# Third query tile, batch 2's scaling and the next queries' loads moved to other places in a linear attention + GEGLU kernel

## The chip, the cores and the metric

The kernel runs on one core of one Trainium2 chip. The metric is the device time of one execution in microseconds (us). Before the change the first three runs had a median of 329.17 us (328.63 to 329.31). The granted TensorE clock was between 0.997 and 1.000.

## The reference

For each of 8 batches and 8 heads (576 tokens of 64 features) a linear attention is computed; its output, laid out as 4,608 tokens of 512 features, goes through a gated feed-forward block.

```python
pos = np.arange(S); theta = np.pi / 2.0 * pos / S          # S = 576
def phi(x): r = np.maximum(x, 0.0); return concat([r * cos(theta), r * sin(theta)], axis=-1)
q_p, k_p = phi(q), phi(k)
kv  = einsum('bhsf,bhsd->bhfd', k_p, v);  z = k_p.sum(axis=2)
x   = einsum('bhsf,bhfd->bhsd', q_p, kv) / (einsum('bhsf,bhf->bhs', q_p, z)[..., None] + 1e-06)
x   = x.transpose(0, 2, 1, 3).reshape(B * S, H * D)        # 4608 x 512
out = (gelu(x @ w_gate) * (x @ w_val)) @ w_out             # 512 -> 1536 -> 512
```

## The kernel before

The feed-forward work is cut into nine blocks of tokens (block 0 has 576, the others 512 or fewer). While block n runs its gate and value matmuls, the attention of batch n + 1 is slipped in between, so that its rows of x are ready for block n + 1. Every engine executes its own instructions in program order, so the place of a call in the program is its place in the engine's queue. These are the pieces that the change moves:

```python
def scale(f, j, which, eng, ...):         # sq(j, which, eng) for queries, sk for keys
    if eng == "v": nc.vector.tensor_scalar(d, s, col, 0.0, op0=ALU.mult, op1=ALU.max)
    else:          nc.scalar.activation(d, s, AF.Relu, scale=col)

def q_by_pe(b, j, bank, eng):             # turn one query tile on TensorE, 8 heads
    ...nc.tensor.transpose(out=qb[:, h, :], in_=qp[:, j, h, :], identity=ident)...
    if eng is not None: q_evac(b, j, bank, eng)     # PSUM -> SBUF on VectorE ("v") or ScalarE ("s")

def norm(xb, bank, g0, g1):               # VectorE: den + eps, reciprocal, numerator * reciprocal
def x_by_pe(b, t, xb, bank, eng):         # turn one tile of x on TensorE, evict it to xT
def turn_x(b, t, xb):                     # the same by a DMA transpose (later batches)

def gate(n, jt, c0, w, gb):               # 4 matmuls into bank gb, then ScalarE: gel = Gelu(bank)
def value(n, jt, c0, w, vb):              # 4 matmuls into bank vb, then VectorE:
    nc.vector.tensor_mul(hT[n % 2][...], gel[:, 0:w], ps[:, vb, 0:w])    # "the product"
```

A value matmul writes bank 6 or 7, and the product on VectorE reads it. The next value matmul into the same bank must wait until that product is done. The start of block 0 before the change:

```python
    x_by_pe(0, 0, x0, 4, "s", 0, 2)
    dummies(2, 5)                         # matmuls that only keep TensorE busy
    x_by_pe(0, 0, x0, 4, "s", 2, 4)
    # [cut]  X(t, ...) is x_by_pe of batch 0; Y(t, ...) is its numerator and norm
    sq(2, 0, "v"), sq(2, 1, "s")
    gate(0, 0, 0, 128, 5)
    gate(0, 1, 0, 128, 4)
    X(1, 2, "s")()
    sq(3, 0, "v"), sq(3, 1, "v")
    dummies(1, 7)
    q_by_pe(0, 2, 3, "v")
    value(0, 0, 0, 128, 6)
    value(0, 1, 0, 128, 7)
    gate(0, 0, 128, 128, 5)
    gate(0, 1, 128, 128, 4)
    sq(4, 1, "s"), sq(4, 0, "v")
    q_by_pe(0, 3, 0, "s")                 # 8 transposes between the gates and the values
    value(0, 0, 128, 128, 6)              # needs the product of value(0, 0, 0, 128, 6)
```

In blocks 1 to 6 small pieces are hung behind the twelve gate-and-value units of a block. In block 1 (n = 1) the attention of batch 2 has its steps after units 5 to 10; step i + 1 ends with the DMA transpose of x tile i. Block 2's first gate reads 448 rows of batch 2, so it needs tile 3, the transpose behind unit 9.

Of the kernel before, what the change touches and what calls it, by code (L numbers as in the profile page):

```python
# [16 lines left out]
def kernel(  # L17
# [12 lines left out]
    B, H, S, D = q.shape  # L30
# [6 lines left out]
    NJ = 4  # L37
# [86 lines left out]
    def dummies(n, bank=7):  # L124
        for _ in range(n):
            nc.tensor.matmul(ps[:, bank, :], lhsT=junk[:, 0:128], rhs=junk, start=True, stop=True)  # L126


    def scale(f, j, which, eng, h0=0, h1=H):
        dst, src = f  # L130
        col = (cos_c if which == 0 else sin_c)[:, j:j + 1]
        s, d = src[:, h0:h1, j, :], dst[:, j, h0:h1, which * D:(which + 1) * D]
        if eng == "v":
            nc.vector.tensor_scalar(d, s, col, 0.0, op0=ALU.mult, op1=ALU.max)  # L134
        else:
            nc.scalar.activation(d, s, AF.Relu, scale=col)  # L136
# [30 lines left out]
    def numer_mm(b, t, bank, g, rows=128):  # L167
        for h in range(4 * g, 4 * g + 4):
            nc.tensor.matmul(  # L169
                ps[0:rows, bank + g, (h % 4) * (D + 1):(h % 4 + 1) * (D + 1)],  # L170
                lhsT=qT[b % 2][:, t, h, 0:rows],
                rhs=kv[b % 2][:, h, 0:D + 1],
                start=True, stop=True,
            )

    def norm(xb, bank, g0, g1, rows=128):

        n = g1 - g0
        nd = ps[0:rows, bank + g0:bank + g1, 0:4 * (D + 1)].rearrange("p g (h e) -> p g h e", e=D + 1)
        den = rot.tile([128, 2, 4], FP32, name="den")  # L180
        nc.vector.tensor_scalar(den[0:rows, 0:n], nd[:, :, :, D], EPS, None, op0=ALU.add)
        rec = rot.tile([128, 2, 4], FP32, name="rec")
        nc.vector.reciprocal(rec[0:rows, 0:n], den[0:rows, 0:n])  # L183
        nc.vector.tensor_tensor(  # L184
            xb[0:rows, g0:g1], nd[:, :, :, 0:D],
            rec[0:rows, 0:n, :, None].to_broadcast([rows, n, 4, D]), op=ALU.mult,
        )
# [4 lines left out]
    def numer(b, t, bank, rows=128):  # L192

        numer_mm(b, t, bank, 0, rows)
        numer_mm(b, t, bank, 1, rows)
        xb = new_xb()
        norm(xb, bank, 0, 2, rows)
        return xb
# [14 lines left out]
    def gate(n, jt, c0, w, gb):  # L213

        p0 = starts[n] + c0
        for ct in range(CT):
            nc.tensor.matmul(  # L217
                ps[:, gb, 0:w], lhsT=wg_sb[:, ct, jt * 128:(jt + 1) * 128],
                rhs=xT[:, ct, p0:p0 + w], start=(ct == 0), stop=(ct == CT - 1),
            )  # L220
        gels[n, jt, c0] = gel = rot.tile([128, 512], FP32, name="gel", bufs=3)
        nc.scalar.activation(gel[:, 0:w], ps[:, gb, 0:w], AF.Gelu)  # L222

    def value(n, jt, c0, w, vb):

        p0 = starts[n] + c0
        for ct in range(CT):
            nc.tensor.matmul(  # L228
                ps[:, vb, 0:w], lhsT=wv_sb[:, ct, jt * 128:(jt + 1) * 128],
                rhs=xT[:, ct, p0:p0 + w], start=(ct == 0), stop=(ct == CT - 1),  # L230
            )
        gel = gels.pop((n, jt, c0))
        nc.vector.tensor_mul(hT[n % 2][:, jt, 64 + c0:64 + c0 + w], gel[:, 0:w], ps[:, vb, 0:w])  # L233

    def gv_unit(n, jt, c0, w, gb, vb, mid=()):
        gate(n, jt, c0, w, gb)
        for f in mid:
            f()
        value(n, jt, c0, w, vb)
# [15 lines left out]
    def o_part(n, m, bank, j0, j1):  # L255
        c0 = 128 * m - starts[n] + 64
        for jt in range(j0, j1):
            nc.tensor.matmul(  # L258
                ps[:, bank, :], lhsT=hT[n % 2][:, jt, c0:c0 + 128], rhs=wo_sb[:, jt, :],
                start=(jt == 0), stop=(jt == JT - 1),  # L260
            )
        if j1 == JT:
            o_store(m, bank)
# [21 lines left out]
    def o_store(m, bank):  # L285
        o_sb = rot.tile([128, C], FP32, name="o_sb", bufs=4)
        nc.scalar.copy(o_sb, ps[:, bank, :])  # L287
        if (128 * m) % S % 128 == 0 and (128 * m) % S < 512:
            nc.sync.dma_start(out=rows_ap(128 * m, 128), in_=o_sb)
        else:  # L290
            nc.sync.dma_start(out=rows_ap(128 * m, 64), in_=o_sb[0:64])
            nc.sync.dma_start(out=rows_ap(128 * m + 64, 64), in_=o_sb[64:128])
# [26 lines left out]
    def q_by_pe(b, j, bank, eng, h0=0, h1=H):  # L319

        qb = ps[:, bank, :].bitcast(BF16).rearrange("p (h t) -> p h t", h=H)
        for h in range(h0, h1):
            nc.tensor.transpose(out=qb[:, h, :], in_=qp[:, j, h, :], identity=ident)  # L323
        if eng is not None:
            q_evac(b, j, bank, eng, h0, h1)

    def q_evac(b, j, bank, eng, h0=0, h1=H):
        qb = ps[:, bank, :].bitcast(BF16).rearrange("p (h t) -> p h t", h=H)
        cp = nc.vector.tensor_copy if eng == "v" else nc.scalar.copy
        if j < NJ:  # L330
            cp(qT[b % 2][:, j, h0:h1], qb[:, h0:h1])  # L331
        else:
            cp(qT[b % 2][:, j, h0:h1, 0:64], qb[:, h0:h1, 0:128:2])

    def x_by_pe(b, t, xb, bank, eng, c0=0, c1=CT, every=1):
        p0 = b * S + t * 128
        cp = nc.vector.tensor_copy if eng == "v" else nc.scalar.copy
        xb2 = xb.rearrange("p g h d -> p (g h d)")
        rows = 128 if t < NJ or every == 2 else 64
        view = ps[:, bank, 0:256].bitcast(BF16).rearrange("p (c t) -> p c t", c=CT)  # L340
        for ct in range(c0, c1):
            nc.tensor.transpose(  # L342
                out=view[:, ct, 0:rows], in_=xb2[0:rows, ct * 128:(ct + 1) * 128], identity=ident[0:rows, 0:rows],
            )
        cp(xT[:, c0:c1, p0:p0 + rows // every], view[:, c0:c1, 0:rows:every])

    def sq(j, which, eng, *h):
        scale(Q, j, which, eng, *h)
# [30 lines left out]
    norm(x0, 6, 0, 1)  # L379
    dummies(1, 4)  # L380
    numer_mm(0, 0, 6, 1)
    norm(x0, 6, 1, 2)
    numer_mm(0, 1, 0, 0)
    numer_mm(0, 1, 0, 1)
    norm(x1, 0, 0, 2)
    x_by_pe(0, 0, x0, 4, "s", 0, 2)
    dummies(2, 5)
    x_by_pe(0, 0, x0, 4, "s", 2, 4)

    nc.gpsimd.tensor_copy(tiny[0:1, 1:2], x0[0:1, 1, 3, D - 1:D])  # L390
    load_w(8, 12)
# [2 lines left out]
    A, Bw = (0, 256), (256, 320)  # L394
    xs = {1: x1}

    def X(t, bank, eng):
        return lambda: x_by_pe(0, t, xs[t], bank, eng)

    def Y(t, bank):  # L400
        def f():
            xs[t] = numer(0, t, bank, 128 if t < NJ else 64)
        return f

    sq(2, 0, "v"), sq(2, 1, "s")
    gate(0, 0, 0, 128, 5)
    gate(0, 1, 0, 128, 4)
    X(1, 2, "s")()
    sq(3, 0, "v"), sq(3, 1, "v")
    dummies(1, 7)  # L410
    q_by_pe(0, 2, 3, "v")
    value(0, 0, 0, 128, 6)
    value(0, 1, 0, 128, 7)
    gate(0, 0, 128, 128, 5)
    gate(0, 1, 128, 128, 4)
    sq(4, 1, "s"), sq(4, 0, "v")
    q_by_pe(0, 3, 0, "s")
    value(0, 0, 128, 128, 6)
    value(0, 1, 128, 128, 7)
    Y(2, 2)()  # L420
    q_by_pe(0, 4, 1, "s")
    gv_unit(0, 2, *A, 4, 6)
    X(2, 0, "s")()
    Y(3, 2)()
# [5 lines left out]
    gv_unit(0, 0, 384, 128, 4, 6)  # L430
    gv_unit(0, 1, 384, 128, 5, 7)
    X(4, 0, "v")()
    gv_unit(0, 4, *A, 3, 1)
    gv_unit(0, 2, *Bw, 4, 6)
    gv_unit(0, 3, *Bw, 5, 7)
    gv_unit(0, 0, 512, 64, 0, 3)
    gv_unit(0, 1, 512, 64, 1, 2)


    load_q(1, nc.gpsimd)  # L440
# [7 lines left out]
    def L(f, *a):  # L448
        return lambda: f(*a)
# [54 lines left out]
    y4 = numer(1, 4, 0)  # L504
    o_part(0, 3, 5, 5, 10)
    x_by_pe(1, 3, y[3], 7, "s")
    o_part(0, 3, 5, 10, 12)
    x_by_pe(1, 4, y4, 6, "v", every=2)

    def attn_step(b, i):  # L510

# [8 lines left out]
    for n in range(1, 7):  # L520
        b = n + 1
        a = after[n]

        def put(u, *fs):
            a[u].extend(fs)

        put(0, L(sq, 0, 0, "v"), L(sq, 1, 0, "v"), L(sq, 1, 1, "v"), L(sq, 0, 1, "s"))
        put(1, L(sq, 2, 0, "v"), L(sq, 2, 1, "s"), L(turn_q, b, 0, 3))
        put(1, L(sq, 3, 0, "v"), L(sq, 4, 0, "v"), L(sq, 4, 1, "v"), L(sq, 3, 1, "s"), L(turn_q, b, 3, 5))
        put(2, L(sk, 0, 0, "v"), L(sk, 1, 0, "v"), L(sk, 0, 1, "s"), L(sk, 1, 1, "s"))  # L530
        put(3, L(sk, 2, 0, "v"), L(sk, 3, 0, "v"), L(sk, 4, 0, "v"))
        put(3, L(sk, 2, 1, "s"), L(sk, 3, 1, "s"), L(sk, 4, 1, "s"), L(cast_v, b, 0, 4))
        put(4, L(cast_v, b, 4, 8, "s"))
        put(5, L(attn_step, b, 0))
        if b + 1 < B:

            for f, u in zip((load_q, load_k, load_v), (3, 4, 5) if n > 1 else (6, 11, 11)):
                put(u, L(f, b + 1))
        for i in range(5):
            put(6 + i, L(attn_step, b, i + 1))  # L540

    for n in range(2, NB):
        for i, m in enumerate(o_tiles_of(n - 1)):
# [47 lines left out]
```

## Time and profile before

| | before |
|---|---|
| median of the first 3 runs | 329.17 us |
| profiled span | 326.8 us |
| PE busy | 97% |
| PE's listed waits after the start-up (0.85 + 0.35 + 0.24 + 0.20) | about 1.6 us |
| the same with the dummy matmul that the change drops (0.22 us) | about 1.9 us |

The part of the page with busy time, share of the span and instruction count of each engine (PE is TensorE's matmuls, PEld its weight loads, DVE VectorE, ACT ScalarE):

```profile
PE 317.6 (97%) x2223; PEld 167.0 (51%) x2223; DVE 171.8 (53%) x382; ACT 150.6 (46%) x270; POOL 21.2 (6%) x41
```

The Trainium skill ("Perfetto Trace Analysis", Identifying the Most-Contended Engine) warns that matmul busy share alone does not tell how close TensorE is to its limit. So the pace is checked as well, in the chain of work that ended last (start in us, us, what, number of instructions):

```profile
60.66 0.86 PE ps L228 x4
61.52 0.86 PE ps L217 x4
```

Four matmuls of 512 columns take 0.86 us, 216 ns each. The Trainium skill ("TensorE: Matmul & The Clock Gate", Back-to-back issue gap) has a formula that for 512 columns comes to 512 / 2.4 + 2.5 = 215.8 ns; it calls this the gap of an isolated matmul, and says that in a stream of weight loads and matmuls the formula counts too much (131 ns measured there). This trace is such a stream, and it runs at 216 ns: the measurement agrees with the formula and not with the 131 ns. The groups shown follow one another without a hole at this pace; here the busy share does mean what it seems to mean. Busy time by stretch (stretch, length, then busy us and instructions of each engine) shows how little is idle once the first blocks are over:

```profile
16.40:25.80 9.40, 9.16 (x144) 8.13 (x144) 8.33 (x26) 6.29 (x16) 3.97 (x6) 1.00 1.30 207
84.00:312.00 228.00, 227.90 (x1409) 110.96 (x1410) 111.04 (x223) 99.31 (x167) 8.63 (x13) 1.00 0.62 149
```

From 84 to 312 us PE is idle 0.1 us of 228. In the first stretch VectorE (third pair of numbers) is busy 8.33 of 9.40 us: in this one place it is nearly as full as PE. What is left to win stands in PE's list of waits (engine, line, what it waited for, us in total, times, longest):

```profile
PE ps L126 <- DVE par_i L103: 1.7, 1, 1.7
PE ps L323 <- ACT qp L136: 1.0, 1, 1.0
PE ps L217 <- DMA xT<-xb: 0.8, 1, 0.8
PE ps L217 <- ACT xT L345: 0.3, 1, 0.3
PE ps L228 <- DVE hT L233: 0.2, 1, 0.2
PE ps L217 <- ACT gel L222: 0.2, 1, 0.2
```

The first two belong to the start-up and the change doesn't touch them. The third is the wait at block 2's first gate, seen in the timeline (start, us, engine, line, operation, tiles, and in brackets the idle time before it and its releaser). SPq is the queue that issues DMAs; the transpose of x tile 3 is issued at 80.96 us, and PE resumes at 83.97 us:

```profile
80.96 1.60 SPq L204 DMA_TRANSPOSE xT<-xb  x1
...
83.97 1.02 PE L217 MATMUL ps<-xT,wg_sb 128*128 128x512 bf16 x4 [0.85 <-DMA xT<-xb]
```

And this is the start of block 0, where the change moves most. (In the timelines of this document only the lines that matter are shown; others between them are left out, also where no dots stand.) DVE L233 is the product, L134 a scaling, L331 the eviction of turned queries; ACT L345 evicts turned x; PE L126 is a dummy, L323 a query turn:

```profile
16.38 0.49 PE L217 MATMUL ps<-xT,wg_sb 128*128 128x128 bf16 x6 [0.35 <-ACT xT L345]
16.94 0.38 PE L126 MATMUL ps<-junk 128*128 128x512 bf16 x1
17.17 0.60 ACT L345 COPY xT<-ps 128x512 bf16<-128x512 bf16 x1
...
18.45 0.47 DVE L233 TENSOR_TENSOR hT<-gel,ps 128x128 bf16<-128x128 f32 x2
18.50 0.61 PE L323 MATMUL ps<-ident,qp 128*128 128x128 bf16 x8
18.94 0.61 PE L228 MATMUL ps<-xT,wv_sb 128*128 128x128 bf16 x8
```

The two first products (x2) run at 18.45 to 18.92 us. PE passes that time with the turn of query tile 3, and its second pair of value matmuls starts at 18.94 us without a wait.

### The profile page before, as it was taken

Reading aid. Unit: us, or ns where it says so; the run is one execution under the profiler, and the core shown is the slowest. Engines: PE = TensorE matmul, PEld = TensorE weight load, DVE = VectorE, ACT = ScalarE, POOL = GpSimd, SP = SyncE. Lnnn points to the kernel's source line nnn. Section 1 sums busy time; section 2 is a strip of 40 time slices with the busy share of each in tenths; the row PEclk is TensorE's granted clock in tenths of the full one; section 3 lists DMA queues with packets and bytes.
Section 4 is the critical chain, followed back from the end, with each engine's and each line's share of the span. In section 5 each row is a group of like instructions: output and inputs, shape, how many; then the busy total and the mean of one; then the engine's idle time right before and its main releaser. Section 6 shows DMA issues by size and latency. Waiting matters only on the chain.

```text
span 326.8 us, 5867 instructions
## 1 busy us (share of the span) xinstructions
PE 317.6 (97%) x2223; PEld 167.0 (51%) x2223; DVE 171.8 (53%) x382; ACT 150.6 (46%) x270; POOL 21.2 (6%) x41
## 2 busy tenths in 40 slices
PE   7799999999899999999999999999999999999994
PEld 3497866555345544544454445444544444444443
DVE  5894776678753667365835484548455222322210
ACT  6574664772474256424652375237622332223321
POOL 2640010000100010001000010001000100100000
PEclk9999999999999999999999999999999999999999
DMA  7999999997699948993699359994523211000024
GB/s 226 284 205 275 205 298 306 316 182 173 189 270 270 299 103 158 301 267 81 129 305 290 81 101 216 357 135 84 144 51 79 44 37 34 32 32 32 35 64 96
DMA packets 87739, 55.42 MB, mean 170 GB/s; under 512 B 52512, under 2 KB 82976, under 8 KB 87712
## 3 DMA queue, kind: packets, MB, share of 16 engines
q1 hardware_dynamic: 81200, 48.71, 60.2%
q0 software_dynamic: 6080, 5.90, 10.1%
q10 hardware_dynamic: 432, 0.46, 0.4%
q8 instruction: 17, 0.28, 0.4%
q14 instruction: 10, 0.08, 0.1%
HBM read 37.75 MB, written 9.44 MB: 144 GB/s over the span
## 4 chain that ended last, share of the span: by engine, by line
PE 93%; DMA 3%; DVE 1%; ACT 1%; issue 1%; POOL 0%; SPq 0%; DVEq 0%; POOLq 0%; ACTq 0%
PE ps L217 28%; PE ps L228 28%; PE ps L258 28%; PE ps L169 3%; PE ps L153 3%; DMA qf<-in_q_dram 2%; PE ps L323 1%; DMA xT<-xb 1%; PE ps L342 1%; PE ps L276 1%; DVE vx L140 0%; SPq L79 0%; DVE hT L233 0%; DVE qT L331 0%; DVE xb L184 0%
## 5 line engine op out<-in xcount | busy, mean ns | idle before, releaser
L233 DVE TENSOR_TENSOR hT<-gel,ps 128x512 bf16<-128x512 f32 (+5 forms) x126 | 76.4, 610 | 129.4 <-PE ps L228 127.8
L217 PE MATMUL ps<-xT,wg_sb 128*128 128x512 bf16 (+5 forms) x504 | 113.7, 348 | 1.4 <-DMA xT<-xb 0.8
L228 PE MATMUL ps<-xT,wv_sb 128*128 128x512 bf16 (+5 forms) x504 | 113.6, 349 | 0.2 <-DVE hT L233 0.2
L222 ACT ACTIVATE gel<-ps 128x512 f32<-128x512 f32 (+5 forms) x126 | 67.5, 536 | 77.6 <-PE ps L217 75.7
L258 PE MATMUL ps<-wo_sb,hT 128*128 128x512 bf16 x420 | 96.5, 379 | 0.0
L228 PEld LDWEIGHTS <-wv_sb 128*128 128x128 bf16 x504 | 47.8, 98 | 46.4 <-issue 0.4
L217 PEld LDWEIGHTS <-wg_sb 128*128 128x128 bf16 x504 | 45.8, 98 | 41.8 <-issue 2.1
L258 PEld LDWEIGHTS <-hT 128*128 128x128 bf16 x420 | 40.0, 98 | 45.4
L287 ACT COPY o_sb<-ps 128x512 f32<-128x512 f32 x35 | 20.5, 586 | 75.2 <-PE ps L258 75.2
L184 DVE TENSOR_TENSOR xb<-ps,rec 128x512 bf16<-128x512 f32 (+2 forms) x41 | 27.8, 678 | 1.7 <-DVE rec L183 0.2
L136 ACT ACTIVATE kp<-kf,sin_c 128x512 bf16<-128x512 f32 (+1 forms) x41 | 25.4, 679 | 0.4 <-DMA kf<-in_k_dram 0.4
L134 DVE TENSOR_SCALAR qp<-qf,cos_c 128x512 bf16<-128x512 f32 x40 | 20.5, 553 | 0.0
L169 PEld LDWEIGHTS <-qT 128*128 128x128 bf16 (+1 forms) x320 | 15.0, 98 | 8.7 <-issue 1.9
L134 DVE TENSOR_SCALAR kp<-kf,cos_c 128x512 bf16<-128x512 f32 (+1 forms) x45 | 18.7, 463 | 1.0 <-DMA kf<-in_k_dram 1.0
L136 ACT ACTIVATE qp<-qf,sin_c 128x512 bf16<-128x512 f32 x27 | 18.5, 712 | 0.0
L169 PE MATMUL ps<-kv,qT 128*128 128x65 bf16 (+1 forms) x320 | 16.5, 193 | 0.2
L208 POOL COPY xT<-xr 128x256 bf16<-128x256 bf16 x6 | 2.4, 403 | 201.0 <-DMA xr<-xb 201.0
L153 PEld LDWEIGHTS <-kp 128*128 128x128 bf16 x320 | 10.9, 97 | 2.6 <-issue 0.7
L126 PE MATMUL ps<-junk 128*128 128x512 bf16 x35 | 9.9, 424 | 1.7 <-DVE par_i L103 1.7
L153 PE MATMUL ps<-vx,kp 128*128 128x65 bf16 x320 | 11.1, 193 | 0.1
L140 ACT CAST vx<-vf 128x1280 bf16<-128x1280 f32 (+1 forms) x9 | 9.7, 1074 | 1.2 <-DMA vf<-in_v_dram 1.2
L244 POOL COPY hT<-hT 128x768 bf16<-128x768 bf16 x8 | 7.6, 948 | 36.8 <-DVE hT L233 36.8
(55 smaller groups left out, 88.9 us busy)
## 6 DMA issues: line engine op xcount, KB each, us to landing
out_dram<-o_sb SPq DMA_DIRECT2D x38, 128.0 KB, 2.4
kf<-in_k_dram SPq DMA_DIRECT2D x7, 640.0 KB, 7.5
out_dram<-o_sb SPq DMA_DIRECT2D x16, 256.0 KB, 3.4
qf<-in_q_dram SPq DMA_DIRECT2D x6, 640.0 KB, 6.2
vf<-in_v_dram SPq DMA_DIRECT2D x6, 640.0 KB, 9.1
kf<-in_k_dram SPq DMA_DIRECT2D x7, 512.0 KB, 6.4
qf<-in_q_dram SPq DMA_DIRECT2D x6, 512.0 KB, 5.4
vf<-in_v_dram SPq DMA_DIRECT2D x6, 512.0 KB, 8.0
```

Source lines behind the costliest of these rows:

```text
L126: nc.tensor.matmul(ps[:, bank, :], lhsT=junk[:, 0:128], rhs=junk, start=True, stop=True)
L134: nc.vector.tensor_scalar(d, s, col, 0.0, op0=ALU.mult, op1=ALU.max)
L136: nc.scalar.activation(d, s, AF.Relu, scale=col)
L153: nc.tensor.matmul(ps[:, bank, (h % 4) * (D + 1):(h % 4 + 1) * (D + 1)], lhsT=kp[:, j, h, :], rhs=vx[b % 2][:, j, h, 0:D + 1], start=(j == ...
L169: nc.tensor.matmul(ps[0:rows, bank + g, (h % 4) * (D + 1):(h % 4 + 1) * (D + 1)], lhsT=qT[b % 2][:, t, h, 0:rows], rhs=kv[b % 2][:, h, 0:D ...
L184: nc.vector.tensor_tensor(xb[0:rows, g0:g1], nd[:, :, :, 0:D], rec[0:rows, 0:n, :, None].to_broadcast([rows, n, 4, D]), op=ALU.mult,)
L217: nc.tensor.matmul(ps[:, gb, 0:w], lhsT=wg_sb[:, ct, jt * 128:(jt + 1) * 128], rhs=xT[:, ct, p0:p0 + w], start=(ct == 0), stop=(ct == CT - 1),
L222: nc.scalar.activation(gel[:, 0:w], ps[:, gb, 0:w], AF.Gelu)
L228: nc.tensor.matmul(ps[:, vb, 0:w], lhsT=wv_sb[:, ct, jt * 128:(jt + 1) * 128], rhs=xT[:, ct, p0:p0 + w], start=(ct == 0), stop=(ct == CT - 1),
L233: nc.vector.tensor_mul(hT[n % 2][:, jt, 64 + c0:64 + c0 + w], gel[:, 0:w], ps[:, vb, 0:w])
L258: nc.tensor.matmul(ps[:, bank, :], lhsT=hT[n % 2][:, jt, c0:c0 + 128], rhs=wo_sb[:, jt, :], start=(jt == 0), stop=(jt == JT - 1),)
L287: nc.scalar.copy(o_sb, ps[:, bank, :])
```

## The change

It has three parts. In block 0's start the third query tile is scaled and turned earlier, in the hole of 0.35 us; the dummy goes; x tile 1 and the turned query tile 4 are evicted by VectorE instead of ScalarE, one scaling goes the other way, the turn of query tile 3 moves behind the value matmuls, and tile 4's gate and value are split. In block 1 a part of batch 2's query scaling is done before the block, and every attention step comes one unit earlier (as do two of the next loads). In blocks 2 to 5 the loads of the next queries go between the two turns of q (block 6 has no next queries to load: `b + 1 < B`).

```diff
--- before.py
+++ after.py
@@ -379,13 +379,16 @@
     norm(x0, 6, 0, 1)
     dummies(1, 4)
     numer_mm(0, 0, 6, 1)
+    sq(2, 1, "s")
     norm(x0, 6, 1, 2)
+    sq(2, 0, "v")
     numer_mm(0, 1, 0, 0)
     numer_mm(0, 1, 0, 1)
     norm(x1, 0, 0, 2)
     x_by_pe(0, 0, x0, 4, "s", 0, 2)
     dummies(2, 5)
     x_by_pe(0, 0, x0, 4, "s", 2, 4)
+    q_by_pe(0, 2, 3, None)
 
     nc.gpsimd.tensor_copy(tiny[0:1, 1:2], x0[0:1, 1, 3, D - 1:D])
     load_w(8, 12)
@@ -402,23 +405,21 @@
             xs[t] = numer(0, t, bank, 128 if t < NJ else 64)
         return f
 
-    sq(2, 0, "v"), sq(2, 1, "s")
     gate(0, 0, 0, 128, 5)
     gate(0, 1, 0, 128, 4)
-    X(1, 2, "s")()
-    sq(3, 0, "v"), sq(3, 1, "v")
-    dummies(1, 7)
-    q_by_pe(0, 2, 3, "v")
+    X(1, 2, "v")()
+    q_evac(0, 2, 3, "v")
+    sq(3, 0, "v"), sq(3, 1, "s")
     value(0, 0, 0, 128, 6)
     value(0, 1, 0, 128, 7)
     gate(0, 0, 128, 128, 5)
     gate(0, 1, 128, 128, 4)
     sq(4, 1, "s"), sq(4, 0, "v")
-    q_by_pe(0, 3, 0, "s")
     value(0, 0, 128, 128, 6)
     value(0, 1, 128, 128, 7)
     Y(2, 2)()
-    q_by_pe(0, 4, 1, "s")
+    q_by_pe(0, 3, 0, "s")
+    q_by_pe(0, 4, 1, "v")
     gv_unit(0, 2, *A, 4, 6)
     X(2, 0, "s")()
     Y(3, 2)()
@@ -430,11 +431,12 @@
     gv_unit(0, 0, 384, 128, 4, 6)
     gv_unit(0, 1, 384, 128, 5, 7)
     X(4, 0, "v")()
-    gv_unit(0, 4, *A, 3, 1)
+    gate(0, 4, *A, 3)
     gv_unit(0, 2, *Bw, 4, 6)
     gv_unit(0, 3, *Bw, 5, 7)
-    gv_unit(0, 0, 512, 64, 0, 3)
-    gv_unit(0, 1, 512, 64, 1, 2)
+    value(0, 4, *A, 1)
+    gv_unit(0, 0, 512, 64, 0, 2)
+    gv_unit(0, 1, 512, 64, 4, 6)
 
 
     load_q(1, nc.gpsimd)
@@ -504,8 +506,11 @@
     y4 = numer(1, 4, 0)
     o_part(0, 3, 5, 5, 10)
     x_by_pe(1, 3, y[3], 7, "s")
+    x_by_pe(1, 4, y4, 6, "v", every=2)
+    for j in range(NJ + 1):
+        sq(j, 0, "v")
     o_part(0, 3, 5, 10, 12)
-    x_by_pe(1, 4, y4, 6, "v", every=2)
+    sq(0, 1, "s")
 
     def attn_step(b, i):
 
@@ -524,20 +529,28 @@
         def put(u, *fs):
             a[u].extend(fs)
 
-        put(0, L(sq, 0, 0, "v"), L(sq, 1, 0, "v"), L(sq, 1, 1, "v"), L(sq, 0, 1, "s"))
-        put(1, L(sq, 2, 0, "v"), L(sq, 2, 1, "s"), L(turn_q, b, 0, 3))
-        put(1, L(sq, 3, 0, "v"), L(sq, 4, 0, "v"), L(sq, 4, 1, "v"), L(sq, 3, 1, "s"), L(turn_q, b, 3, 5))
-        put(2, L(sk, 0, 0, "v"), L(sk, 1, 0, "v"), L(sk, 0, 1, "s"), L(sk, 1, 1, "s"))
-        put(3, L(sk, 2, 0, "v"), L(sk, 3, 0, "v"), L(sk, 4, 0, "v"))
-        put(3, L(sk, 2, 1, "s"), L(sk, 3, 1, "s"), L(sk, 4, 1, "s"), L(cast_v, b, 0, 4))
-        put(4, L(cast_v, b, 4, 8, "s"))
-        put(5, L(attn_step, b, 0))
+        s = 0 if n > 1 else -1
+        if n > 1:
+            put(0, L(sq, 0, 0, "v"), L(sq, 1, 0, "v"), L(sq, 1, 1, "v"), L(sq, 0, 1, "s"))
+            put(1, L(sq, 2, 0, "v"), L(sq, 2, 1, "s"), L(turn_q, b, 0, 3))
+            put(1, L(sq, 3, 0, "v"), L(sq, 4, 0, "v"), L(sq, 4, 1, "v"), L(sq, 3, 1, "s"))
+            if b + 1 < B:
+                put(1, L(load_q, b + 1))
+            put(1, L(turn_q, b, 3, 5))
+        else:
+            put(0, L(sq, 1, 1, "s"), L(sq, 2, 1, "v"), L(turn_q, b, 0, 3))
+            put(0, L(sq, 3, 1, "v"), L(sq, 4, 1, "s"), L(turn_q, b, 3, 5))
+        put(2 + s, L(sk, 0, 0, "v"), L(sk, 1, 0, "v"), L(sk, 0, 1, "s"), L(sk, 1, 1, "s"))
+        put(3 + s, L(sk, 2, 0, "v"), L(sk, 3, 0, "v"), L(sk, 4, 0, "v"))
+        put(3 + s, L(sk, 2, 1, "s"), L(sk, 3, 1, "s"), L(sk, 4, 1, "s"), L(cast_v, b, 0, 4))
+        put(4 + s, L(cast_v, b, 4, 8, "s"))
+        put(5 + s, L(attn_step, b, 0))
         if b + 1 < B:
 
-            for f, u in zip((load_q, load_k, load_v), (3, 4, 5) if n > 1 else (6, 11, 11)):
+            for f, u in ((load_k, 3), (load_v, 5)) if n > 1 else ((load_q, 5), (load_k, 10), (load_v, 11)):
                 put(u, L(f, b + 1))
         for i in range(5):
-            put(6 + i, L(attn_step, b, i + 1))
+            put(6 + s + i, L(attn_step, b, i + 1))
 
     for n in range(2, NB):
         for i, m in enumerate(o_tiles_of(n - 1)):
```

## The prediction

> **What bounds the kernel now.** TensorE. The table of engines shows PE busy 317.6 of 326.8 us (97%), VectorE 53%, ScalarE 46%. In the chain of waits four matmuls of 512 columns take 0.864 us, 216 ns each. The Trainium skill ("TensorE: Matmul & The Clock Gate", Back-to-back issue gap) gives columns / 2.4 GHz + 2.5 ns, 215.8 ns; the trace agrees. From 84 to 312 us (busy time by stretch) PE is idle 0.1 us of 228. Only idle PE time elsewhere can be won.
>
> PE's list of waits: 1.7 us at the start and 1.0 us for the first scaled queries (untouched), 0.35 us at 16.4 us for ScalarE's eviction of turned x, 0.24 us at 25.2 and 0.20 us at 29.6 us for PSUM banks, and 0.85 us at 84.0 us, where block 2's first gate matmul waits for a DMA transpose of batch 2 (2.88 us, landing 83.8). With the removed dummy matmul (0.22 us) the change can reach about 1.9 us, 0.6%.
>
> **What the change does.**
> 1. Block 1 (batch 2). Query scaling partly goes before the block: five VectorE scalings of 0.48 us and one on ScalarE (0.71 us), where VectorE has idle time. The attention steps move one unit earlier, 1.7 us (gate and value) to 2.0 us (with a numerator). The transpose that landed too late should land over 1 us early. Gain 0.85 us, on the path. VectorE's first product is delayed about 0.5 us, inside the double-buffered banks' slack. The last x transpose, moved before two output matmuls, may wait 0.1 us for its input.
>
> 2. Block 0 start. The third query tile is turned earlier, filling the 0.35 us hole and removing a dummy. But VectorE is nearly full from 16.5 to 25 us, and its queue is in order. It gets x tile 1's eviction (0.42 us) and tile 4's query eviction (about 0.4 us), gives up one scaling (0.47 us), and does one scaling before tile 1's normalization, which ends near 17.1 instead of 16.6 us. My hand estimate from these durations: the first two products come at 19.0-19.5 instead of 18.45-18.9 us. The next value matmuls need their banks, and without the query turn that stood there, PE waits up to 0.8 us at about 18.5 us. Net, PE is about 0.3 us later at 21 to 26 us (range 0.3 earlier to 0.7 later). Tile 4's split gate and value trades the 0.20 us wait at 29.6 us for a similar one behind a product: nothing.
>
> 3. Later blocks: the next queries' loads (issue 1.3 us) go between the two turns of q. The second turn is delayed a few us, but is first used at unit 9, over 10 us later; PE waited for no load there. Value: zero.
>
> **Prediction.** -0.85 + 0.1 + 0.3 = -0.45 us: 328.7 us, 8 in 10 between 327.6 and 329.7. Faster by over 2%: 0.5%; within 2%: 98.5%; slower: 1%.
>
> **What would show it.** PE's wait for the x transpose at 84 us is gone. Between 17 and 26 us PE shows new waits of 0.3 to 1 us on VectorE's products, and block 0's output matmuls (now at 45.3 us) begin 0 to 0.6 us later. Batch 2's transposes issue 1.5 to 2 us earlier. Afterwards PE is as gapless as before, 216 ns a matmul, clock near 1.00.
>
> **What would make it wrong.** If VectorE keeps up at 17 to 20 us, hole and dummy are both won and the time falls by up to 1.9 us. If the loads beside the second query turn delay the transposes of x past a block's start, waits on DMA of 1 us or more appear in blocks 2 to 6. If batch 2's queries land after about 60 us, VectorE stalls at the start of block 1.

## The result, and the profile after

In the first four runs the changed kernel had a median of 328.95 us (328.66 to 329.21) against 328.90 us before (4 runs), ratio 1.0001, 95% interval 0.9984 to 1.0019. A ratio is the mean time of one kernel's fast runs over the mean of the other's in the same rounds, so it isn't quite the ratio of the medians that are quoted. Five more runs (the eighth experiment) gave 328.87 against 328.82 us, ratio 1.0000, interval 0.9986 to 1.0013. The kernel is as fast as before. The predicted 328.7 us lies 0.2 us away, inside the runs' spread. Part of this closeness is luck: the forecast was a drop of 0.45 us from 329.17 us, the kernel before came out at 328.90 us in the result's rounds, and the measured difference is +0.05 us.

The busy line of the page after:

```profile
PE 316.1 (97%) x2188; PEld 167.1 (51%) x2222; DVE 172.2 (53%) x383; ACT 150.5 (46%) x269; POOL 21.6 (7%) x41
```

A trap lies here. PE seems to have 35 matmuls and 1.5 us less. The program dropped only one matmul, the dummy, as the count of weight loads shows (2,222 for 2,223). The other 34 records are missing from this trace; a second trace of the same program had all 2,222, and 318.3 us busy. So I compare where instructions start, not busy sums. PE's list of waits after:

```profile
PE ps L126 <- DVE par_i L103: 1.7, 1, 1.7
PE ps L323 <- ACT qp L136: 1.3, 1, 1.3
PE ps L228 <- DVE hT L233: 0.8, 2, 0.6
PE ps L169 <- DVE xb L184: 0.3, 1, 0.3
```

The wait for the transpose of x and those for ScalarE (the eviction of x, a Gelu) are gone. In their place stand 0.8 us behind VectorE's products (0.56 of it new) and 0.3 us of a numerator matmul behind VectorE's normalization, which nobody had forecast. The timeline of block 0's start:

```profile
16.52 0.45 PEld L323 LDWEIGHTS <-qp 128*128 128x128 bf16 x8 [0.28 <-DVE qp L134]
16.52 0.62 PE L323 MATMUL ps<-ident,qp 128*128 128x128 bf16 x8
16.81 0.69 DVE L184 TENSOR_TENSOR xb<-ps,rec 128x512 bf16<-128x512 f32 x1
17.56 0.40 PE L342 MATMUL ps<-ident,xb 128*128 128x128 bf16 x4
17.99 0.42 DVE L345 COPY xT<-ps 128x512 bf16<-128x512 bf16 x1 [0.49 <-PE ps L342]
18.33 0.68 DVE L331 COPY qT<-ps 128x1024 bf16<-128x1024 bf16 x1
...
18.93 0.48 DVE L134 TENSOR_SCALAR qp<-qf,cos_c 128x512 bf16<-128x512 f32 x1
19.32 0.48 DVE L233 TENSOR_TENSOR hT<-gel,ps 128x128 bf16<-128x128 f32 x2
19.65 0.61 PE L228 MATMUL ps<-xT,wv_sb 128*128 128x128 bf16 x8 [0.56 <-DVE hT L233]
```

VectorE now has eviction, eviction, scaling and only then the products, back to back from 17.99 us. Just before, it is not busy but blocked: the normalization of x tile 1 (L184) ends at 17.50 us, and VectorE stands idle for 0.49 us, because next in its order is the eviction of x tile 1, which PE (L342) turns only at 17.56 us. The query eviction behind it could have run, since its turn on PE was over. The value matmuls at 19.65 us then wait 0.56 us. Nor is the old hole really filled: the query turn's weight loads waited 0.28 us for its scaling on VectorE, and start at 16.52 us. Now block 2's first gate; nothing stands in brackets:

```profile
80.53 1.38 SPq L204 DMA_TRANSPOSE xT<-xb  x1
...
84.26 1.03 PE L217 MATMUL ps<-xT,wg_sb 128*128 128x512 bf16 x4
```

And the place of the new numerator wait, in block 1:

```profile
71.26 1.03 PE L228 MATMUL ps<-xT,wv_sb 128*128 128x512 bf16 x4
71.46 0.60 ACT L222 ACTIVATE gel<-ps 128x512 f32<-128x512 f32 x1 [0.49 <-PE ps L217]
72.76 0.69 DVE L233 TENSOR_TENSOR hT<-gel,ps 128x512 bf16<-128x512 f32 x1 [2.23 <-PE ps L169]
...
74.54 0.42 PE L169 MATMUL ps<-kv,qT 128*128 128x65 bf16 x8 [0.27 <-DVE xb L184]
```

The value matmuls end at 71.26 + 1.03 = 72.29 us and the Gelu at 72.06 us, so the product could start at about 72.35 us. It starts at 72.76 us, with VectorE idle. The bracket names a matmul that the product does not need, which is how this view looks when no recorded event explains a start. In the trace, the product's wait for PE is passed at 72.33 us, and then nothing happens for 0.43 us.

To see where time comes and goes without the scatter of the first loads, I cut each trace at four points: the start of the second group of kv matmuls (A), block 0's first output matmul (B), block 1's first gate (C), block 2's first gate (D), and the last matmul (E). All times are PE start times in the trace. D is taken as the start of block 2's first output matmul less the 3.455 us of four gapless groups before it.

| kernel | A at | A to B | B to C | C to D | D to E |
|---|---|---|---|---|---|
| before | 13.08 | 32.27 | 14.29 | 24.34 | 238.20 |
| after | 13.57 | 32.71 | 14.29 | 23.70 | 238.20 |
| after, second trace | 13.07 | 32.72 | 14.29 | 23.69 | 238.21 |

In these traces the start of block 0 lost 0.44 us, block 1 won 0.64 us, the rest is unchanged. That makes -0.20 us, which the timed runs can't tell from zero. The later start A in the first trace (0.49 us) is not the change's: up to there both programs are the same, and over all thirteen traces A lies between 12.85 and 13.70 us without regard to the kernel.

The listed waits don't add up to the 0.44 us: a wait of 0.56 us came, a hole of 0.35 us and a dummy of 0.22 us went. The list counts from modelled ends. So I count from one matmul's start to the next, beyond the usual step (56 ns for 128 columns), and leave out what is the same in both. Before the change the old hole is then 0.51 us, a second one 0.11 us, and the dummy 0.22 us. After it there are 0.27 us ahead of the query turn, 0.13 us ahead of x tile 1's turn, 0.24 us ahead of the next gates, which need x tile 1's eviction, and 0.72 us ahead of the value matmuls. That is 0.84 against 1.36 us; of these 0.52 us, 0.44 us are left at B.

### The profile page after: what moved, and what is told of

Its sections match the earlier page's. It is cut to its first block, busy times and chain, and to the rows that moved or that the text cites. A ratio compares the mean times of both kernels' runs of the same rounds, so it can differ in the third digit from the quotient of the medians.

```text
span 327.1 us, 5831 instructions
## 1 busy us (share of the span) xinstructions
PE 316.1 (97%) x2188; PEld 167.1 (51%) x2222; DVE 172.2 (53%) x383; ACT 150.5 (46%) x269; POOL 21.6 (7%) x41
## 4 chain that ended last, share of the span: by engine, by line
PE 91%; DVE 3%; DMA 2%; issue 1%; SPq 1%; POOL 0%; ACT 0%; DVEq 0%; POOLq 0%
PE ps L217 28%; PE ps L258 28%; PE ps L228 27%; PE ps L169 3%; PE ps L153 3%; DMA vf<-in_v_dram 2%; SPq L79 1%; DVE hT L233 1%; PE ps L276 1%; PE ps L342 1%; PE ps L323 1%; DVE xb L184 1%; DVE qp L134 0%; DVE rec L183 0%; DVE vx L140 0%
## 5 line engine op out<-in xcount | busy, mean ns | idle before, releaser
L228 PE MATMUL ps<-xT,wv_sb 128*128 128x512 bf16 (+5 forms) x492 | 111.8, 348 | 1.1 <-DVE hT L233 0.8
L217 PE MATMUL ps<-xT,wg_sb 128*128 128x512 bf16 (+5 forms) x490 | 111.8, 348 | 1.0
L258 PE MATMUL ps<-wo_sb,hT 128*128 128x512 bf16 x413 | 95.5, 379 | 0.6
L184 DVE TENSOR_TENSOR xb<-ps,rec 128x512 bf16<-128x512 f32 (+2 forms) x41 | 27.8, 678 | 1.7 <-DVE rec L183 0.2
L136 ACT ACTIVATE qp<-qf,sin_c 128x512 bf16<-128x512 f32 x28 | 19.3, 712 | 0.0
```

Of the source, the lines that this page charges most:

```text
L184: nc.vector.tensor_tensor(xb[0:rows, g0:g1], nd[:, :, :, 0:D], rec[0:rows, 0:n, :, None].to_broadcast([rows, n, 4, D]), op=ALU.mult,)
L217: nc.tensor.matmul(ps[:, gb, 0:w], lhsT=wg_sb[:, ct, jt * 128:(jt + 1) * 128], rhs=xT[:, ct, p0:p0 + w], start=(ct == 0), stop=(ct == CT - 1),
L228: nc.tensor.matmul(ps[:, vb, 0:w], lhsT=wv_sb[:, ct, jt * 128:(jt + 1) * 128], rhs=xT[:, ct, p0:p0 + w], start=(ct == 0), stop=(ct == CT - 1),
L258: nc.tensor.matmul(ps[:, bank, :], lhsT=hT[n % 2][:, jt, c0:c0 + 128], rhs=wo_sb[:, jt, :], start=(jt == 0), stop=(jt == JT - 1),)
```

## The experiments

The theory: VectorE's full in-order queue costs at block 0's start what block 1 wins, and the loads do nothing. Rivals: the start is a gain and the loss lies elsewhere (in the loads or in the scatter of the first loads); or the loss at the start comes only from the missing query turn. A second question came up on the way: what makes the product in block 1 late. The first expectations give D to E up to the start of the last tile's group of matmuls (235.69 us before), 2.51 us before the last matmul.

All eleven runs gave the right result. The table has all of them; "median" is of five runs, and the kernel before had nine runs beside them.

| run | median us | before us | ratio (95%) | A to B | C to D | D to E |
|---|---|---|---|---|---|---|
| 1 start only | 329.31 | 328.89 | 1.0013 (1.0000 to 1.0027) | 32.70 | 24.50 | 238.20 |
| 2 block 1 only | 328.33 | 328.89 | 0.9984 (0.9971 to 0.9996) | 32.28 | 23.71 | 238.21 |
| 3 loads only | 329.06 | 328.89 | 1.0004 (0.9991 to 1.0016) | 32.26 | 24.12 | 238.21 |
| 4 x tile 1 on ScalarE | 327.65 | 328.89 | 0.9961 (0.9948 to 0.9973) | 32.12 | 23.33 | 238.01 |
| 5 after, one more VectorE op | 328.53 | 328.82 | 0.9993 (0.9980 to 1.0005) | 32.71 | 23.34 | 238.55 |
| 6 run 4, one more VectorE op | 328.09 | 328.82 | 0.9980 (0.9968 to 0.9993) | 32.13 | 23.70 | 238.21 |
| 7 run 4, x tile 4 later | 327.44 | 328.82 | 0.9957 (0.9945 to 0.9970) | 32.04 | 23.33 | 238.42 |
| 8 after again | 328.87 | 328.82 | 1.0000 (0.9986 to 1.0013) | 32.72 | 23.69 | 238.21 |
| 9 run 4, old loads | 327.47 | 328.67 | 0.9964 (0.9951 to 0.9978) | 32.13 | 23.33 | 238.01 |
| 10 run 4 again | 327.41 | 328.67 | 0.9962 (0.9950 to 0.9975) | 32.12 | 23.33 | 238.01 |
| 11 after, query turn back | 328.93 | 328.67 | 1.0010 (0.9998 to 1.0023) | 32.85 | 23.70 | 238.21 |

### Runs 1 to 3: each part alone

Each is the kernel before with one part of the change: for run 1 all hunks up to the one with `value(0, 4, *A, 1)`; for run 2 the scalings before block 1 and, with n = 1, the units moved by one; for run 3, with n > 1:

```diff
-        put(1, ..., L(sq, 3, 1, "s"), L(turn_q, b, 3, 5))
+        put(1, ..., L(sq, 3, 1, "s"))
+        if n > 1 and b + 1 < B:
+            put(1, L(load_q, b + 1))
+        put(1, L(turn_q, b, 3, 5))
-            for f, u in zip((load_q, load_k, load_v), (3, 4, 5) if n > 1 else (6, 11, 11)):
+            for f, u in ((load_k, 3), (load_v, 5)) if n > 1 else ((load_q, 6), (load_k, 11), (load_v, 11)):
```

> Only the block 0 part of the change. Theory (VectorE's in-order queue makes PE wait for products): from the second group of kv matmuls to block 0's first output matmul PE takes 32.7 us as in the changed kernel, against 32.26 us before (+0.4), with one wait of about 0.56 us on a product near 19 us after the start; the 0.85 us wait for the x transpose at block 2's start stays. Time +0.4 us, ratio 1.0013. Rival (the third query tile's early turn wins hole and dummy, 0.5 us, and the loss in the changed kernel lies elsewhere): 31.8 us or less, ratio 0.998 to 0.999. The second kv group starts anywhere from 13.0 to 13.7 us if that is only the landing of the first loads (theory), at 13.5 us or later if the change causes it (rival).

> Only the batch 2 and block 1 part. Theory: block 0 as before (32.26 us from the second kv group to the first output matmul), from block 1's first gate to block 2's first gate 23.5 to 23.7 us against 24.34 us before, so 0.6 to 0.85 us less; no wait for the x transpose at block 2; perhaps the new wait of 0.27 us of a numerator matmul on VectorE. Time -0.65 us, ratio 0.998. Rival (the moved scalings only shift the wait, or the loads eat it): 24.3 us and ratio 1.000.

> Only the loads of the next queries between the two turns of q in blocks 2 to 6. Theory: PE has no waits from block 2 to the end, 228 us from block 2's first gate to the end as before within 0.1 us; ratio 1.000. Rival (the loads collide with the transposes and cost what block 1 wins): PE waits on DMA of 0.5 us or more after block 2's start, ratio 1.002 or more.

Run 1 was 0.42 us slower in the medians (its interval just touches 1) and its first stretch 32.70 us; the wait of 0.56 us is in its trace, and so is the one at block 2 (1.01 us there). Its A was 12.85 us, the earliest of all, so the change does not cause the late A either. Run 2 was 0.56 us faster, C to D 23.71 us. Run 3 is not to be told from before; D to E is unchanged. The sum of the three differences, 0.42 - 0.56 + 0.17, is 0.03 us, and the whole change measured 0.05 us. So it is a gain and a loss of about the same size, in different blocks, and the theory of the start holds, that of VectorE's queue; what the queue was late with is shown by run 4. The DMA wait at block 2 moves by itself between executions: 0.85 us before, 1.01 in run 1, 0.64 in run 3.

### Run 4: one eviction back on ScalarE

```diff
-    X(1, 2, "v")()
+    X(1, 2, "s")()
```

> The whole change with one engine changed back: x tile 1's eviction on ScalarE. Theory: VectorE reaches the first two products about 0.4 us earlier, so PE's wait of 0.56 us near 19 us falls to 0.1 to 0.3 us (x tile 1 is ready 0.2 us later on ScalarE, which gives some of it back), and from the second kv group to block 0's first output matmul PE takes 32.3 to 32.5 us instead of 32.7. Rival (the wait comes only from the missing query turn between gate and value, not from VectorE's queue): wait and stretch unchanged within 0.1 us. Ratio 0.998 to 0.9995.

The time fell by 1.24 us against the kernel before, more than any theory had expected. Two things happened. The first is the expected one, larger; in this timeline the products come at 17.86 us and the second pair of value matmuls at 18.52 us does not wait at all:

```profile
17.45 0.59 ACT L345 COPY xT<-ps 128x512 bf16<-128x512 bf16 x1
17.86 0.48 DVE L233 TENSOR_TENSOR hT<-gel,ps 128x128 bf16<-128x128 f32 x2
18.08 0.61 PE L217 MATMUL ps<-xT,wg_sb 128*128 128x128 bf16 x8 [0.23 <-ACT xT L345]
...
18.52 0.61 PE L228 MATMUL ps<-xT,wv_sb 128*128 128x128 bf16 x8
```

ScalarE takes 0.59 us for the eviction and VectorE 0.42 us, yet the kernel is faster with the slower engine, because ScalarE had the room and VectorE no longer stands blocked: from the start of tile 1's normalization to that of the query eviction it takes 0.61 us here (16.26 to 16.87) and 1.52 us in the changed kernel (16.81 to 18.33). Of these 0.91 us the eviction itself is 0.34 us, start to start; 0.57 us is VectorE standing in front of it. No run left the eviction on VectorE but behind the query eviction, so it stays open whether the order alone would have done. By starts PE's hole ahead of the gates at 18.08 is 0.39 us instead of 0.24, and that of 0.72 us ahead of the value matmuls is gone. From A to B it is 32.12 us, 0.6 us less than after. The second thing was not expected: C to D fell from 23.70 to 23.33 us and D to E from 238.20 to 238.01 us, in blocks that the edit doesn't touch. The late product in block 1 was on time here:

```profile
70.14 1.03 PE L228 MATMUL ps<-xT,wv_sb 128*128 128x512 bf16 x4
71.27 0.69 DVE L233 TENSOR_TENSOR hT<-gel,ps 128x512 bf16<-128x512 f32 x1 [1.86 <-PE ps L228]
```

The value matmuls end at 71.17 us, the product starts 0.10 us later. I then counted VectorE's records in the traces, waits on semaphores included. The kernels before, after and runs 1 to 3 have 577, and in each the 192nd, the 320th and the 448th record starts 0.42 to 0.45 us after the record before it, where the same pair of operations elsewhere takes 0.07 us (a product after its wait) or 0.22 us (a normalization). In the kernel before and runs 1 and 3, the 192nd record is another product, one that waits for its Gelu anyway, so only about 0.15 us of the lateness shows there. Run 4 has one record less, and none is late. That is a theory of position: the lateness sits at every 128th place in VectorE's stream, and what stands there decides whether PE feels it.

### Runs 5 and 6: one VectorE instruction more

Both add the same tiny operation where VectorE is idle, before the first keys land: run 5 to the whole change (578 records), run 6 to run 4 (577 again).

```diff
     nc.vector.tensor_mul(sin_c[:, NJ:NJ + 1], sin_c[:, NJ:NJ + 1], even)
+    pad = sb.tile([1, 8], FP32, name="pad")
+    nc.vector.memset(pad, 0.0)
```

> The whole change plus one tiny VectorE memset in its idle time before the first keys land; nothing else differs. Theory (position): in all four kernels with 577 VectorE records the 192nd, 320th and 448th record starts 0.2 to 0.4 us late with nothing in the trace to wait for; in the kernel with 576 none is late. One more record puts a semaphore wait, long anyway, at place 192, so the product in block 1 is on time: block 1's first gate to block 2's first gate 23.33 us instead of 23.70, and no wait of a numerator matmul on VectorE there. At place 320 comes a wait that follows a reciprocal at once, so that lateness should stay (block 2's first gate to the last tile 235.69 us). Time -0.37 us against the changed kernel, ratio to before about 0.999. Rival (chance, or the loads in flight): 23.70 us as before.

> The kernel with x tile 1 evicted on ScalarE, with the same tiny VectorE memset, so 577 records again. Theory (position): the late starts come back at records 192, 320 and 448: block 1 takes 23.70 us instead of 23.34, block 2 to the end 235.69 instead of 235.50, the numerator's wait of 0.27 us is there; the start stays 32.1 to 32.3 us. Ratio to before 0.9975 to 0.998 instead of 0.996. Rival (ScalarE's eviction itself made those gains): ratio 0.996 and 23.34 us.

Line numbers are two higher in these kernels. In run 5 the product is on time; in run 6 it is late again, and the numerator waits again:

```profile
72.11 0.69 DVE L235 TENSOR_TENSOR hT<-gel,ps 128x512 bf16<-128x512 f32 x1 [1.87 <-PE ps L230]
```

```profile
71.57 0.69 DVE L235 TENSOR_TENSOR hT<-gel,ps 128x512 bf16<-128x512 f32 x1 [2.24 <-PE ps L171]
...
73.35 0.41 PE L171 MATMUL ps<-kv,qT 128*128 128x65 bf16 x8 [0.28 <-DVE xb L186]
```

C to D is 23.34 us with the extra operation on the whole change and 23.70 us with it on run 4: the effect goes either way with the count of records, while the eviction's engine is held fixed. The stretch repeats: of the ten traces with the moved steps, the five with 577 records have 23.69 to 23.71 us and the five with 576 or 578 have 23.33 or 23.34 us. So chance and the loads in flight are out, and so is the place of the tiles in memory, which `pad` could shift: run 5 and run 6 both have it, and only run 6 is late. The timed runs agree but would not show it alone: run 5 won 0.34 us against run 8 (medians 328.53 and 328.87, same rounds; their intervals overlap), 0.37 us was expected; run 6 lost 0.0019 in ratio against run 4 (other rounds, intervals overlap narrowly), about 0.6 us, where 0.37 us in block 1 and 0.20 us in D to E were expected. One part of run 5's expectation failed: I had expected the lateness to stay at place 320, and no record is late there. Its D to E is longer all the same, because in that one execution PE waited 0.37 us for a DMA transpose of x at 218.66 us.

### Run 7: another VectorE queue point

The wait of 0.23 us of a value matmul near 25 us stands behind the normalization of x tile 4. So that goes one unit later.

```diff
-    Y(4, 2)()
     gv_unit(0, 1, 256, 128, 5, 7)
+    Y(4, 2)()
```

> The kernel with x tile 1 evicted on ScalarE, and the numerator of tile 4 with its normalization one gate and value later. The wait of 0.23 us of a value matmul near 25 us stood behind that normalization on VectorE; it should go: from the second kv group to block 0's first output matmul 31.9 us instead of 32.13. The rest as in that kernel. Ratio to before 0.995 to 0.9965. If the wait only moves to the transpose of x tile 4, no change.

The value matmul no longer waits, but the transpose of x tile 4 now does, for 0.27 us. A to B fell by only 0.08 us, not by 0.23: the wait moved, as the last sentence of the expectation allowed. In the timed runs its interval overlaps that of run 4 almost wholly; a gain is not shown.

### Run 8: the changed kernel again

No edit.

> The changed kernel itself, once more, for a narrower interval: ratio 0.9995 to 1.0005. The sum of its parts' ratios (1.0013, 0.9984, 1.0004) gives 1.0001. The second kv group's start, 13.08 us before and 13.57 us in its first trace, should fall anywhere between 12.8 and 13.7 us, as first loads land; the stretches 32.70, 14.29, 23.70 and 235.69 us should repeat within 0.05 us.

The stretches repeated within 0.02 us, A was 13.07 us, and the ratio 1.0000.

### Runs 9 and 10: do the loads matter in the better kernel?

Run 9 is run 4 with `load_q` at unit 3 and `load_k` at unit 4 for n > 1, as before the change; run 10 is run 4 unchanged, beside it.

> The kernel with x tile 1 evicted on ScalarE, with the loads of blocks 2 to 6 in their old places. Theory (the loads' new places bring nothing, and leave the x transposes of a later block less room at its start: the first x transpose of block 2 is issued at 106.6 to 107.4 us with the new places and 104.4 to 106.2 with the old, and two traces with the new places had a wait on an x transpose at 117 or 219 us): as fast as the kernel with the new places or faster by up to 0.3 us, ratio 0.995 to 0.996; no such wait in the trace. Rival (the new places help): slower than it by 0.3 us or more.

> The kernel with x tile 1 evicted on ScalarE once more, beside the last one on the same chip: ratio to before 0.996 (0.9955 to 0.9965); stretches 32.1, 14.29 and 23.33 us as in its first trace; block 2's first gate to the last matmul 238.0 us, or up to 0.6 us more where a wait on an x transpose falls in.

Medians 327.47 and 327.41 us, every stretch equal within 0.01 us. The places of the loads are worth nothing, in either direction, at the size that these runs can see (0.1% or so). Waits on a transpose of x at a later block's start turned up in two of thirteen traces (0.25 us at 116.82 us in run 7, 0.37 us in run 5); both kernels had the new places, but other traces with the new places had none, so whether those places cause them stays open.

### Run 11: the query turn back as a filler

```diff
     sq(4, 1, "s"), sq(4, 0, "v")
+    q_by_pe(0, 3, 0, "s")
     value(0, 0, 128, 128, 6)
     value(0, 1, 128, 128, 7)
     Y(2, 2)()
-    q_by_pe(0, 3, 0, "s")
```

> The whole change with one thing undone: the turn of query tile 3 stands again before the second pair of value matmuls, where it filled PE's time in the kernel before. Theory (VectorE's queue is late, not only the filler missing): the query turn itself then waits about 0.4 us for its VectorE scaling, so nothing is won: second kv group to block 0's first output matmul 32.6 to 32.9 us against 32.70. Rival (the missing filler is the cause): 32.2 to 32.3 us as before the change, ratio 0.9985.

```profile
18.49 0.47 DVE L134 TENSOR_SCALAR qp<-qf,cos_c 128x512 bf16<-128x512 f32 x1
...
19.11 0.61 PE L323 MATMUL ps<-ident,qp 128*128 128x128 bf16 x8 [0.46 <-DVE qp L134]
19.55 0.61 PE L228 MATMUL ps<-xT,wv_sb 128*128 128x128 bf16 x8
```

The value matmuls no longer wait, but the query turn waits 0.46 us for its scaling, which comes late from the same queue. A to B is 32.85 us, worse than the 32.71 of the change. The missing filler was not the cause; VectorE's queue was.

## Why the prediction was right, point by point

- **What bounds the kernel, and the ceiling of 1.9 us.** Right. Even the best kernels here (run 4 and its repeat, 1.24 and 1.26 us faster in the medians, and run 7, 1.38 us) stayed below it.
- **Block 1, -0.85 us.** Right in mechanism; the size was off: -0.64 us. The wait for the transpose went, and the transposes are issued 1.36 us earlier against the block's start (the last at 19.97 instead of 21.33 us after it), less than the 1.5 to 2 us forecast. Two things were wrong in the term. The list of waits counts from the modelled end of the last matmul, the way that I read 0.85 us; by the starts in the first trace the hole at block 2 was 1.01 us (83.97 less the start of the four matmuls before it, 82.10, and their usual 0.86 us), and 1.01 us is also what the moved steps win against this trace where nothing else interferes (24.34 to 23.33 or 23.34 us, runs 4, 5, 7, 9 and 10). Runs 1 and 3, with the same old block 1, took 24.50 and 24.12 us, so the hole is 0.8 to 1.2 us from one execution to the next. And the term lacked the late product at VectorE's 192nd record: by the starts it opened a hole of 0.37 us ahead of the numerator (0.44 us after the changed kernel's preceding matmuls, 0.07 us before), shown by runs 5 and 6. 1.01 - 0.37 is the 0.64 us measured between these two traces; against runs 1 and 3 the same block wins 0.80 and 0.42 us.
- **Block 0's start, +0.3 us.** Right in the main mechanism: VectorE's in-order queue, and a wait of the value matmuls for their banks. Shown by runs 1, 4 and 11. It measured +0.44 us; the wait was 0.56 us, inside "up to 0.8 us". Two parts of the term were wrong. It counted the hole of 0.35 us as filled, but the query turn itself waited 0.28 us for its scaling. And it called VectorE nearly full and charged x tile 1's eviction with its 0.42 us alone; the trace shows VectorE idle for 0.49 us in front of it.
- **The x transpose before the last output matmuls, +0.1 us.** Wrong but small: B to C is 14.28 or 14.29 us in every trace.
- **Tile 4's split gate and value: nothing.** Right: from the value matmuls before it (25.23 before, 26.21 after) to the next full gate (29.65 and 30.58) is 4.42 us before and 4.37 after.
- **Loads between the turns: zero.** Right, by run 3 and by runs 9 and 10. The second turn of q in block 2 was indeed delayed, its issue ended at 100.70 us instead of 97.17, and nothing waited for it.
- **The sum, -0.45 us.** By the stretches it is -0.20 us, by the timed runs 0.0 with an interval of about 0.4 us to either side; the forecast change lies at the edge of that interval. The terms measured -0.64 (forecast -0.85), +0.44 (+0.3) and 0.00 (+0.1). The one most mis-sized is the first: I took a listed wait that ends for time that is won, and the engine that stood next in line (VectorE, for the numerator) gave 0.37 us back.

Open: what makes each 128th VectorE record late. The Trainium skill ("Perfetto Trace Analysis", The 4-stage abstract model) says that an instruction has 64 bytes and that fetching and decoding precede the wait; the page of the profile shows instruction transfers by DMA of 8 KB each (10 of them, 0.08 MB, on one queue). 128 instructions of 64 bytes are 8 KB, an estimate from the skill's 64 bytes. It would fit if VectorE stood at the border of two such pieces, and if the lateness showed only where the instruction before is a short wait that can't hide it. The times of these transfers stand in the packed traces, and they rule out the plainest form, that VectorE waits for one to arrive: at none of the 24 late records (three in each of the eight traces with 577) was an instruction transfer under way, the last one of 8 KB had ended at least 9 us before, and the next began 0.2 to 4.8 us after the record. What happens on the chip at such a border no run measured; this part is argued, not shown. Shown are the places, and that one record more or less moves the effect.

## What to carry to other kernels

When the main engine is 97% busy, every hole that is filled has an engine behind it that fills it: cost that engine's queue at that very place, in order, and not its average share of the span (VectorE was 53% busy overall and 89% there, 8.33 of 9.40 us). Ask of each operation also when its input is ready: one that must wait holds up all that stands behind it (0.57 us here, more than its own 0.34). A helper operation that runs faster on the fuller engine can be better placed on the slower, emptier one. And when an edit moves time in blocks that it doesn't touch, look for starts that no event explains, and test whether they follow the count of instructions in the queue: one idle instruction more can be a cheap experiment.

## What the Trainium skill lacked or had wrong

- No page has the late start at every 128th VectorE record: 0.42 to 0.45 us after a wait where 0.07 us (a product) or 0.22 us (a normalization) is usual, at records 192, 320 and 448 of every kernel with 577 records, none in the kernels with 576 or 578. It would belong to "Runtime: NRT & Kernel Launch", Instruction fetch mechanics, if the cause lies in fetching, and else to "Perfetto Trace Analysis".
- "VectorE: DVE Perf Modes", Specifications, says that ScalarE sits closer to PSUM and VectorE closer to SBUF. Here the same eviction of a 128x512 bf16 tile from PSUM took 0.42 us on VectorE and 0.59 us on ScalarE, so for this tile nearness to PSUM did not tell which engine evicts faster.
- "Perfetto Trace Analysis" doesn't say that matmul records can be missing: two traces of the same program had 2,188 and 2,222 matmuls, and 316.1 and 318.3 us of busy time. The weight loads were complete (2,222) in both.
- No page tells how much the landing of the first loads scatters: the first operation that waits for queries ran at 8.76 to 9.63 us in thirteen traces of programs that are the same up to there, save one tiny operation in two of them.
